# Softmax tiles of a two-block attention kernel stored as two halves, and a later place for some loads

## The chip, the cores and the metric

One NeuronCore of one Trainium2 chip runs the whole kernel. The metric is device time in microseconds (us) for one execution. The kernel before was run three times: 259.44, 259.83 and 260.8 us, median 259.83 us. Its engines are named as the profile names them: PE (TensorE matmul), PEld (its weight load), DVE (VectorE), ACT (ScalarE), POOL (GpSimd) and SP (SyncE, which here issues every DMA of the kernel).

## What is computed

Two attention blocks over 2048 tokens of width 640, with 32 heads of 20 elements, side by side in the output. All inputs are bfloat16.

```python
def _A_ref(x, wqkv, wo):          # block A: sliding window of 256 keys
    q, k, v = ...                 # x @ wqkv, cut in three, 32 heads of 20
    scores = jnp.einsum("bhqd,bhkd->bhqk", q, k) * (Dh ** -0.5)
    mask = (idx[:, None] - idx[None, :] >= 0) & (idx[:, None] - idx[None, :] < W)   # W = 256
    p = _softmax(jnp.where(mask[None, None], scores, -1e9), axis=-1)
    return einsum("bhqk,bhkd->bhqd", p, v) (heads joined) @ wo

def _B_ref(x, wqkv, wo):          # block B: linear attention
    pq, pk = phi(q), phi(k)       # phi(t) = where(t > 0, t + 1, exp(t)) + 1e-6
    kv = jnp.einsum("bhsd,bhse->bhde", pk, v)
    z = jnp.einsum("bhsd->bhd", pk)
    o = einsum(pq, kv) / (einsum(pq, z) + 1e-6)
    return (heads joined) @ wo
```

## The kernel before, in words

**Superblocks and tiles.** The 2048 tokens are cut into 4 superblocks s of 512 queries. Block A works on groups of 4 heads (8 groups g). The function `tiles_of` (L39) packs the needed parts of the banded score matrix of one superblock into score tiles of 128 keys by 4 heads by 512 columns: 16 tiles for superblock 0, 20 for each of the others, 76 in all, numbered 0 to 75. From superblock 1 on, five tiles serve two groups g and h = g+1, in this order: `first(g)`; `before(g)` with `middle(g)`; `last(g)` with `middle(h)`; `first(h)`; `before(h)` with `last(h)`. In a tile with two pieces, the first piece fills columns 0 to 255 of every head and the second columns 256 to 511. So the third tile of five holds, in one buffer, a half that group g needs (`last`) and a half that only group h needs later (`middle`, called "M").

**One tile** is made by `scores` (L753). PE multiplies keys and queries into a PSUM tile `S_ps` (L763; one buffer, half of PSUM). ACT takes the exponential of all 4 x 512 columns into the SBUF tile `p` (L781; five buffers). POOL then sets to zero what lies outside the window, with affine selects (L795): one of 128 columns a head for each "D" or "E" edge, and two of 256 columns a head for "M", the first of which writes another tile, `plow`, and the second `p` itself.

**values** (L806) multiplies a group's tiles with the values of block A: for every piece four matmuls (L822), one for each head j = 0 to 3, which run side by side in four column strips of the array and read `columns(p, j, ...)`. It is issued two tiles (LAG) after the group's last tile. Pieces of `first` are read as four runs of 64 columns with a step of 128 (`step=P`); all others as one run.

**Filling PE.** Between tiles, PE gets the dense matmuls of both blocks (projections, key sums, output products) from a plan written out by hand. Each entry has a due time t in tiles: `at(t0, t1, ...)` spreads the banks of a product over t0 to t1, `do(t, t, ...)` places a call. `fill_of` (L1058) sorts all entries by t, and the main loop (L1084) takes columns from that list as each tile gives it credit. In the profile tile i starts about 18 + 3 i us after the span's start (tile 27 at 97.1 us, tile 34 at 118.0 us). A load takes no PE columns, so moving one changes SP's order and nothing in the order of the other engines.

**SP's order** is the program's order, and SP stands still at an entry whose operand isn't ready. These calls matter below: `load_part` (L934, a DMA transpose of 128 tokens of x into `xA` or `xB`, 4 for a superblock, 160 KB each), `load_tok` (L535, 640 KB of block B's tokens), `keep_x` (L927, writes the transposed `xB`, 640 KB, to DRAM scratch `x_scr`), `again_x` (L930, reads it back), `late_load` (L969; "B", 0 is 800 KB of query weights into `wB`), and `moves` (L369): the projected queries and keys of a superblock are partly written to scratch (L375) and read back in another place (L384), 4 writes and 4 reads of 60 KB for each.

Each p buffer, as `scores` makes it:

```python
p_all = pp.tile([P, 4 * SB + 2], BF16, name="p")
p = p_all[:, 0 : 4 * SB].rearrange("p (j q) -> p j q", j=4)
```

Of the kernel before, what the change touches and what calls it, by code (L numbers as in the profile page):

```python
# [11 lines left out]
ACT = mybir.ActivationFunctionType  # L12
# [8 lines left out]
SB = 512  # L21
# [13 lines left out]
HALF = P // 2  # L35
LOW = 2 * P
# [46 lines left out]
def columns(t, j, col, n, step):  # L83

    if step == HALF:
        return t[:, j, col : col + n]
    u = col % step
    v = t[:, j, col - u : col - u + n // HALF * step].rearrange("p (b q) -> p b q", q=step)
    return v[:, :, u : u + HALF]


@with_exitstack
def kernel(
# [10 lines left out]
    nc = tc.nc  # L104
# [4 lines left out]
    scale = float(DH) ** -0.5  # L109
# [127 lines left out]
    def soon(fn, banks):  # L237
        posts.append((begun[0] + banks, fn))
        posts.sort(key=lambda p: p[0])

    def settle(all=True):
        while posts and (all or posts[0][0] <= begun[0]):
            posts.pop(0)[1]()
# [4 lines left out]
    def add_load(a=0, d=0):  # L248
        load["A"] += a
        load["D"] += d  # L250
# [71 lines left out]
    for c in range(KT):  # L322
        m = EXTRA * c
        while m < EXTRA * (c + 1):
            n = min(EXTRA * (c + 1) - m, DH - m % DH)
# [424 lines left out]
    def key(s, rel):  # L750
        return 4 * s + rel

    def scores(s, parts, selects):  # L753
        S_ps = sps.tile([P, 4, SB], F32, name="S_ps")
        p_all = pp.tile([P, 4 * SB + 2], BF16, name="p")
        p = p_all[:, 0 : 4 * SB].rearrange("p (j q) -> p j q", j=4)
        nc.scalar.activation(out=p_all[0:1, 4 * SB : 4 * SB + 1], in_=ident[0:1, 0:1], func=ACT.Copy)

        def product(g, kb, k0, k1, q0, n, col, step):
            kt = k_pad[kb // TPS]  # L760
            ko = (kb % TPS) * P
            for j in range(4):
                nc.tensor.matmul(  # L763
                    columns(S_ps[k0:k1], j, col, n, step),
                    lhsT=kt[32 * j : 32 * j + DH, g, ko + k0 : ko + k1],
                    rhs=q_pad[s][32 * j : 32 * j + DH, g, q0 : q0 + n],
                    start=True,
                    stop=True,
                    tile_position=(32 * j, k0),
                )  # L770

        for g, rel, q0, n, col, step in parts:
            if rel == "M":
                own = key(s, q0 // P)
                product(g, own, 0, HALF, q0, n, col, step)

                far = own - 2 if own >= 2 else own
                product(g, far, HALF, P, q0 + (HALF if own >= 2 else 0), n, col, step)
            else:
                product(g, key(s, rel), 0, P, q0, n, col, step)  # L780
        nc.scalar.activation(out=p, in_=S_ps[:], func=ACT.Exp, scale=scale)  # L781
        add_load(a=2080)
        low = None
        if any(kind == "M" for kind, _, _ in selects):
            low = pl_.tile([P, 4, LOW], BF16, name="plow")
        for kind, c0, n in selects:

            v = p[:, :, c0 : c0 + n].rearrange("p j (b q) -> p j b q", q=HALF)
            if kind == "M":
                lv = low[:, :, c0 - LOW : c0 - LOW + n].rearrange("p j (b q) -> p j b q", q=HALF)  # L790
                jobs = [(lv, v, 1, 0), (v, v, -1, -HALF - 1)]
            else:
                jobs = [(v, v, 1, HALF) if kind == "D" else (v, v, -1, -1)]
            for dst, src, sgn, base in jobs:
                nc.gpsimd.affine_select(  # L795
                    out=dst,
                    in_=src,
                    pattern=[[0, 4], [0, n // HALF], [sgn, HALF]],
                    compare_op=ALU.is_ge,
                    fill=0.0,  # L800
                    base=base,
                    channel_multiplier=-sgn,
                )
        return p, low

    def values(s, g, held):  # L806


        O_ps = dps.tile([P, SB], F32, name="dense")
        todo = []  # L810
        for (_, rel, q0, n, col, step), (p, low) in held:
            if rel == "M":
                own = key(s, q0 // P)
                todo.append((own, low, q0, n, col - LOW, step))
                if own >= 2:
                    todo.append((own - 2, p, q0 + HALF, n, col, step))
            else:
                todo.append((key(s, rel), p, q0, n, col, step))
        for i, (kb, p, q0, n, col, step) in enumerate(todo):
            at = (kb % TPS * H + 4 * g) * HV  # L820
            for j in range(4):
                nc.tensor.matmul(  # L822
                    O_ps[32 * j : 32 * (j + 1), q0 : q0 + n],
                    lhsT=v_flat[kb // TPS % 3][:, at + j * HV : at + j * HV + 32],
                    rhs=columns(p, j, col, n, step),
                    start=(i == 0),
                    stop=(i == len(todo) - 1),
                    tile_position=(0, 32 * j),
                    skip_group_check=True,
                )  # L830
        if turns[0] and g == 0:
            settle()

        T = tp.tile([P, SB // 32, 32], F32, name="T")
        nc.vector.transpose(out=T.rearrange("p b e -> p (b e)"), in_=O_ps[:])  # L835
        add_load(d=1500)
        if s not in norm_A:
            norm_A[s] = (
                np_.tile([P, SB // 32, P], BF16, name="N"),
                np_.tile([P, SB // 32, 32], BF16, name="Nr"),  # L840
            )
        N, Nr = norm_A[s]

        def rest():
            r = sp.tile([P, SB // 32, 1], F32, name="recA")
            nc.vector.reciprocal(out=r[:], in_=T[:, :, DH:HV])
            lo = g * DH
            for dst, a, b in ((N, lo, min(lo + DH, P)), (Nr, max(lo, P), lo + DH)):
                if a >= b:
                    continue  # L850
                at = a - P if dst is Nr else a
                nc.vector.tensor_tensor(  # L852
                    out=dst[:, :, at : at + b - a],
                    in0=T[:, :, a - lo : b - lo],
                    in1=r[:].to_broadcast([P, SB // 32, b - a]),
                    op=ALU.mult,
                )
            if lo < P <= lo + DH:
                oT_A[s] = op1.tile([P, KT, SB], BF16, name="oT")

                def turn(j):
                    quadrant = slice(32 * j, 32 * (j + 1))
                    nc.sync.dma_start_transpose(
                        out=oT_A[s][:, j, :].rearrange("p (b e) -> p b e", e=32),
                        in_=N[quadrant].rearrange("p b x -> p (b x)"),
                    )
                    turns[0] -= 1

                if s < NS - 1:
                    turns[0] = 4  # L870
                    for j in range(4):
                        soon(lambda j=j: turn(j), 2 + 2 * j)
            if g == NG - 1:
                nc.vector.transpose(
                    out=oT_A[s][:, KT - 1, :], in_=Nr.rearrange("p b e -> p (b e)")
                )

        later.append((begun[0], rest))
# [48 lines left out]
    def keep_x(s):  # L927
        nc.sync.dma_start(out=x_scr[s], in_=xB[s].rearrange("p k n -> p (k n)"))
# [73 lines left out]
    def at(t0, t1, gen, n):  # L1002
        for i in range(n):
            plan.append((t0 + (i + 0.5) / n * (t1 - t0), gen, i == n - 1))

    def do(t0, t1, fns):
        fns = list(fns)
        for i, fn in enumerate(fns):
            plan.append((t0 + (i + 0.5) / len(fns) * (t1 - t0), None, fn))
# [22 lines left out]
        at(t0, t1, b_keys(s), KT)  # L1032
    for half, t0, t1 in ((0, 16.4, 21.5), (1, 33.6, 39.2)):
        at(t0, t1, b_sums(half), KT + 2)
    for s, t in ((0, 6), (1, 11), (2, 23), (3, 24)):
        do(t, t, [lambda s=s: load_tok(s)])
    at(40.4, 42, b_kv(), 2)
    do(42.8, 44.8, [lambda c=c: kv_ready(c) for c in range(3)])
# [6 lines left out]
    for n, s, t0, t1 in (("A", 0, 44.5, 48.5), ("A", 1, 49.2, 54.2), ("B", 0, 55.2, 59.4),  # L1045
                         ("B", 1, 60.2, 64), ("A", 2, 64.4, 68.2), ("B", 2, 69, 73),
                         ("B", 3, 73, 76)):
        at(t0, t1, (a_out if n == "A" else b_out)(s), KT)
    for n, s, t0, t1 in (("B", 1, 5, 9), ("A", 2, 6, 12), ("B", 2, 14, 18), ("A", 3, 16, 24),
                         ("B", 3, 17, 22)):  # L1050
        parts(t0, t1, n, s)
    for s, t0, t1 in ((0, 2, 33.5), (1, 12, 38.5), (2, 20, 45.5), (3, 26, 51.2)):
        do(t0, t0, [lambda s=s: keep_x(s)])
        do(t1, t1, [lambda s=s: again_x(s)])
    for t, n, w in ((13, "B", 2), (20, "B", 0), (40.6, "A", A_wo), (42, "B", B_wo)):
        do(t, t, [lambda n=n, w=w: late_load(n, w)])

    def fill_of(events):  # L1058
# [25 lines left out]
    for i, (s, parts, selects, done) in enumerate(units):  # L1084
        p = scores(s, parts, selects)
# [60 lines left out]
```

## Time and profile before

| what | before |
| --- | --- |
| runs, median (range) | 259.83 us (259.44 to 260.8) |
| the profiled execution's own time | 260.06 us |
| its span, first to last instruction | 258.3 us |
| PE busy | 248.4 us, 96% of the span |
| ACT, DVE, POOL busy | 200.2, 176.9, 171.6 us |
| granted TensorE clock | 1.0 |
| bytes moved by DMA | 36.35 MB, mean 141 GB/s |

The profiled execution spends 1.8 us outside its span. Busy shares are of the span. A line number such as L822 is one of the kernel before. "Idle before" an instruction is the time in which its engine did nothing just ahead of it, and "<-" names what ended that time. The chain is the sequence of work that ended last, followed back from the end.

### The profile page before, as it was taken

The page shows a single profiled execution, that of the slowest core. Times are in us where ns is not written, and L with a number is a line of the kernel's source. Part 1 is how long each engine was busy: PE and PEld are TensorE (multiplying, and loading weights), DVE is VectorE, ACT ScalarE, POOL GpSimd, SP SyncE. Part 2 cuts the span into 40 slices and gives each one's busy share as a digit, 9 for nine tenths or more (in the row PEclk, how much of TensorE's full clock was granted, in tenths as well). Part 3 has the DMA queues.
Part 4 walks back from the last instruction along what each step waited for, and adds up shares of the span by engine and source line. Part 5 has one row for each costly group of instructions (what it writes and reads, how often), then busy time and mean ns, then how long its engine had stood idle before and what let it go on. Part 6 is the DMA issues. An engine that isn't in the chain of part 4 may idle for free.

```text
span 258.3 us, 10761 instructions
## 1 busy us (share of the span) xinstructions
PE 248.4 (96%) x4722; PEld 143.0 (55%) x4769; DVE 176.9 (68%) x308; ACT 200.2 (77%) x260; POOL 171.6 (66%) x211
## 2 busy tenths in 40 slices
PE   8999999999999999999999999999999999999995
PEld 7644446556555745555457555555556454555573
DVE  0435787786735457866645677699999879978662
ACT  3466878899777788988667887788889998988742
POOL 7214777767794866758495787949667694976800
PEclk9999999999999999999999999999999999999999
DMA  6995588789869592403474591622957486985715
GB/s 204 323 240 157 94 207 125 153 217 213 114 93 265 113 289 38 147 3 60 95 110 124 69 179 43 171 44 58 181 91 167 66 174 171 103 141 122 232 48 184
DMA packets 65012, 36.35 MB, mean 141 GB/s; under 512 B 48197, under 2 KB 63941, under 8 KB 64965
## 3 DMA queue, kind: packets, MB, share of 16 engines
q1 hardware_dynamic: 64965, 35.67, 65.2%
q8 instruction: 37, 0.61, 1.0%
q14 instruction: 10, 0.08, 0.1%
HBM read 14.42 MB, written 9.83 MB: 94 GB/s over the span
## 4 chain that ended last, share of the span: by engine, by line
PE 85%; POOL 6%; issue 4%; ACT 3%; DVE 1%; ACTq 0%; DVEq 0%
PE dense L277 44%; PE S_ps L763 11%; PE dense L546 9%; PE dense L822 8%; PE dense L412 8%; POOL p L795 4%; ACT p L781 2%; POOL plow L795 2%; PE dense L197 1%; PE dense L653 1%; PE dense L696 1%; PE dense L178 1%; PE dense L625 1%; ACT e L287 1%; DVE phi L294 1%
## 5 line engine op out<-in xcount | busy, mean ns | idle before, releaser
L781 ACT ACTIVATE p<-S_ps 128x2048 bf16<-128x2048 f32 x76 | 142.4, 1873 | 34.0 <-PE S_ps L763 33.2
L795 POOL TENSOR_SCALAR_AFFINE_SELECT p<-p 128x512 bf16<-128x512 bf16 (+1 forms) x152 | 123.2, 821 | 64.0 <-ACT p L781 58.7
L277 PE MATMUL dense<-xA,wqk 128*128 128x512 bf16 x183 | 47.2, 379 | 1.1 <-issue 0.6
L795 POOL TENSOR_SCALAR_AFFINE_SELECT plow<-p 128x1024 bf16<-128x1024 bf16 x32 | 38.7, 1210 | 2.2
L763 PE MATMUL S_ps<-qpad,kpad 20*64 20x64 bf16 (+3 forms) x1728 | 35.2, 213 | 0.4
L763 PEld LDWEIGHTS <-kpad 20*64 20x64 bf16 (+1 forms) x1728 | 17.4, 100 | 30.0 <-issue 25.5
L835 DVE STREAM_TRANSPOSE T<-dense 128x512 f32<-128x512 f32 x32 | 22.8, 712 | 12.5 <-PE dense L822 12.4
L277 PEld LDWEIGHTS <-wqk 128*128 128x128 bf16 x200 | 18.5, 98 | 20.6 <-issue 1.3
L291 DVE TENSOR_SCALAR e<-e 128x512 bf16<-128x512 bf16 x40 | 22.0, 550 | 10.7 <-ACT e L287 10.2
L294 DVE SCALAR_TENSOR_TENSOR phi<-dense,e 128x512 bf16<-128x512 f32 x40 | 27.7, 691 | 1.5
L412 PE MATMUL dense<-wA,xA 128*128 128x320 bf16 x160 | 28.4, 306 | 0.1
L822 PE MATMUL dense<-p,vA 128*32 128x64 bf16 (+2 forms) x1152 | 27.1, 223 | 0.5 <-POOL p L795 0.4
L277 PE MATMUL dense<-wB,xB 128*128 128x128 bf16 (+1 forms) x156 | 25.4, 297 | 0.8 <-issue 0.6
L287 ACT ACTIVATE e<-dense 128x512 bf16<-128x512 f32 x40 | 23.4, 594 | 2.5 <-PE dense L277 2.2
L277 PE MATMUL dense<-wo,oT 128*128 128x128 bf16 (+2 forms) x154 | 24.3, 296 | 1.0 <-issue 0.6
L546 PE MATMUL dense<-phi,tok 128*128 128x128 bf16 (+1 forms) x154 | 24.3, 296 | 0.7 <-issue 0.3
L277 PE MATMUL dense<-xB,wB 128*128 128x512 bf16 x90 | 24.2, 380 | 0.6 <-issue 0.3
L822 PEld LDWEIGHTS <-vA 128*32 128x32 bf16 x1664 | 22.2, 96 | 3.5 <-issue 1.3
L277 PE MATMUL dense<-wB,xA 128*128 128x512 bf16 (+1 forms) x156 | 23.4, 297 | 0.5 <-issue 0.3
L852 DVE TENSOR_TENSOR N<-T,recA 128x320 bf16<-128x320 f32 (+1 forms) x28 | 18.7, 668 | 3.3 <-DMA oT<-N 2.4
L732 DVE TENSOR_TENSOR tok<-tok,rden 128x640 bf16<-128x640 bf16 x16 | 19.8, 1236 | 0.0
L412 PEld LDWEIGHTS <-xA 128*128 128x128 bf16 x160 | 14.8, 100 | 9.0 <-issue 1.1
(68 smaller groups left out, 238.2 us busy)
## 6 DMA issues: line engine op xcount, KB each, us to landing
out_dram<-osb SPq DMA_DIRECT2D x7, 640.0 KB
x_scr<-xB SPq DMA_DIRECT2D x4, 640.0 KB
tok<-in_B_x_dram SPq DMA_DIRECT2D x4, 640.0 KB
xB<-x_scr SPq DMA_DIRECT2D x4, 640.0 KB
wB<-in_B_wqkv_dram SPq DMA_DIRECT2D x3, 800.0 KB
q_scr<-qpad SPq DMA_DIRECT2D x16, 60.0 KB
k_scr<-kpad SPq DMA_DIRECT2D x16, 60.0 KB
qpad<-q_scr SPq DMA_DIRECT2D x16, 60.0 KB
```

What stands on the lines that cost most here:

```text
L277: nc.tensor.matmul(dst, lhsT=lhs(kt), rhs=rhs(kt), start=(kt == 0), stop=(kt == KT - 1))
L287: nc.scalar.activation(out=view(e), in_=src, func=ACT.Exp)
L291: nc.vector.tensor_scalar(out=e[:], in0=e[:], scalar1=1e-6, scalar2=1.0 + 1e-6, op0=ALU.add, op1=ALU.min)
L294: nc.vector.scalar_tensor_tensor(out=dst, in0=src, scalar=0.0, in1=view(e), op0=ALU.max, op1=ALU.add)
L412: nc.tensor.matmul(ps[:, 0 : hh * DH], lhsT=xt[:, kt, tb * P : (tb + 1) * P], rhs=w_sb["A"][:, kt, i * hh * DH : (i + 1) * hh * DH], start ...
L546: nc.tensor.matmul(out, lhsT=lhs(x, pk)[:, tb, :], rhs=rhs(pk, tb), start=(i == 0), stop=(i == len(blocks) - 1),)
L732: nc.vector.tensor_tensor(out=vh, in0=vh, in1=rden_of[s][:, tb, :, :].to_broadcast([P, H, DH]), op=ALU.mult)
L763: nc.tensor.matmul(columns(S_ps[k0:k1], j, col, n, step), lhsT=kt[32 * j : 32 * j + DH, g, ko + k0 : ko + k1], rhs=q_pad[s][32 * j : 32 * ...
L781: nc.scalar.activation(out=p, in_=S_ps[:], func=ACT.Exp, scale=scale)
L795: nc.gpsimd.affine_select(out=dst, in_=src, pattern=[[0, 4], [0, n // HALF], [sgn, HALF]], compare_op=ALU.is_ge, fill=0.0, base=base, chan ...
L822: nc.tensor.matmul(O_ps[32 * j : 32 * (j + 1), q0 : q0 + n], lhsT=v_flat[kb // TPS % 3][:, at + j * HV : at + j * HV + 32], rhs=columns(p, ...
L835: nc.vector.transpose(out=T.rearrange("p b e -> p (b e)"), in_=O_ps[:])
```

## The change

The tile `p` keeps its size, but its columns are ordered differently. Before, head j had its 512 columns in one piece (head, column). After, columns 0 to 255 of all four heads come first, then columns 256 to 511 of all four heads (half, head, column). The exponential writes in the new order, the selects and the matmuls of `values` address it through the half; `plow` and `S_ps` are as before, so the list in `values` carries for each piece the function that addresses it. Besides, entries of the plan get other due times.

```diff
+def columns_p(t, j, col, n, step):
+    if step == HALF:
+        return t[:, col // LOW, j, col % LOW : col % LOW + n]
+    v = t[:, :, j, :].rearrange("p a (b q) -> p a b q", q=step)
+    return v[:, :, :, col : col + HALF]
...
-        p = p_all[:, 0 : 4 * SB].rearrange("p (j q) -> p j q", j=4)
+        p = p_all[:, 0 : 4 * SB].rearrange("p (a j q) -> p a j q", a=2, j=4)
...
-        nc.scalar.activation(out=p, in_=S_ps[:], func=ACT.Exp, scale=scale)
+        nc.scalar.activation(
+            out=p.rearrange("p a j q -> p j a q"),
+            in_=S_ps.rearrange("p j (a q) -> p j a q", a=2),
+            func=ACT.Exp,
+            scale=scale,
+        )
...
-            v = p[:, :, c0 : c0 + n].rearrange("p j (b q) -> p j b q", q=HALF)
+            v = p[:, c0 // LOW, :, c0 % LOW : c0 % LOW + n].rearrange(
+                "p j (b q) -> p j b q", q=HALF
+            )
...
-                todo.append((own, low, q0, n, col - LOW, step))
+                todo.append((own, low, q0, n, col - LOW, step, columns))
                 if own >= 2:
-                    todo.append((own - 2, p, q0 + HALF, n, col, step))
+                    todo.append((own - 2, p, q0 + HALF, n, col, step, columns_p))
             else:
-                todo.append((key(s, rel), p, q0, n, col, step))
-        for i, (kb, p, q0, n, col, step) in enumerate(todo):
+                todo.append((key(s, rel), p, q0, n, col, step, columns_p))
+        for i, (kb, p, q0, n, col, step, of) in enumerate(todo):
...
-                    rhs=columns(p, j, col, n, step),
+                    rhs=of(p, j, col, n, step),
...
-    for s, t in ((0, 6), (1, 11), (2, 23), (3, 24)):
+    for s, t in ((0, 6), (1, 11), (2, 24.2), (3, 28.2)):
         do(t, t, [lambda s=s: load_tok(s)])
...
-    for n, s, t0, t1 in (("B", 1, 5, 9), ("A", 2, 6, 12), ("B", 2, 14, 18), ("A", 3, 16, 24),
-                         ("B", 3, 17, 22)):
+    for n, s, t0, t1 in (("B", 1, 5, 9), ("A", 2, 6, 12), ("B", 2, 14, 18), ("B", 3, 19, 25),
+                         ("A", 3, 25.5, 33.5)):
         parts(t0, t1, n, s)
-    for s, t0, t1 in ((0, 2, 33.5), (1, 12, 38.5), (2, 20, 45.5), (3, 26, 51.2)):
+    for s, t0, t1 in ((0, 2, 33.5), (1, 12, 38.5), (2, 26.2, 45.5), (3, 30.2, 51.2)):
         do(t0, t0, [lambda s=s: keep_x(s)])
         do(t1, t1, [lambda s=s: again_x(s)])
-    for t, n, w in ((13, "B", 2), (20, "B", 0), (40.6, "A", A_wo), (42, "B", B_wo)):
+    for t, n, w in ((13, "B", 2), (32.2, "B", 0), (40.6, "A", A_wo), (42, "B", B_wo)):
         do(t, t, [lambda n=n, w=w: late_load(n, w)])
```

## Prediction, made before the changed kernel was run

> **What bounds the kernel now.** I read the page's busy row first, then the chain, the waits of PE, PE's timeline around the longest ones, POOL's part of the chain there, and last the stretches that tell what the DMA engines did.
>
> ```profile
> span 258.3 us, 10761 instructions
> PE 248.4 (96%) x4722; PEld 143.0 (55%) x4769; DVE 176.9 (68%) x308; ACT 200.2 (77%) x260; POOL 171.6 (66%) x211
> PE 85%; POOL 6%; issue 4%; ACT 3%; DVE 1%; ACTq 0%; DVEq 0%
> ```
>
> PE is busy nearly throughout, at the full granted clock, and 85% of the chain is PE. So only two things can move the end: PE's own work, or the few places where PE stands. All of PE's waits:
>
> ```profile
> PE dense L277 <- issue: 2.5, 16, 0.2
> PE dense L197 <- DVE osb L193: 1.1, 1, 1.1
> PE dense L822 <- POOL p L795: 0.4, 2, 0.3
> PE dense L546 <- issue: 0.3, 2, 0.2
> PE dense L277 <- DVE wB L264: 0.3, 1, 0.3
> ```
>
> Columns: who waited for whom, us in all, times, longest. No row names a DMA. The 1.1 us is the start. What remains with a releaser that the change touches is POOL's, 0.4 us in two waits; the wait is longer than that row says, because a matmul counts as busy till its modelled end. PE's timeline at one of the two places, and the chain there (start us, us, what):
>
> ```profile
> 211.13 0.22 PE L822 MATMUL dense<-p,vA 128*32 128x64 bf16 x5
> 211.62 0.29 PE L822 MATMUL dense<-p,vA 128*32 128x64 bf16 x7 [0.26 <-POOL p L795]
> ```
>
> ```profile
> 208.74 1.16 POOL plow L795
> 209.90 0.06 issue
> 209.96 1.62 POOL p L795
> 211.58 0.04 issue
> 211.62 0.29 PE dense L822 x7
> ...
> 225.29 1.62 POOL p L795
> 226.91 0.04 issue
> 226.96 0.29 PE dense L822 x7
> ```
>
> The reader is to see that the stop falls inside a set of four. `values` of an even group issues 48 matmuls for `first`, `before` and `middle`, and then the 64-column piece of `last`, heads 0 to 3. Four of the row x5 are the end of `middle`, the fifth is head 0 of `last`; head 1 starts only when a select of 1.62 us ends. That length is the form of 1024 elements (0.67 us is the 512 form's median), so PE waits for the second select of "M", which writes columns 256 to 511 of the same tile. These matmuls read columns 0 to 63. Head 0 needn't wait for it (its columns lie ahead of all that "M" writes), but heads 1 to 3 lie between the "M" columns of head 0 and those of head 3: the wait is taken for the whole stretch of memory from the select's first to its last element. In every `values` of an even group from superblock 1 on, the 49th and the 50th matmul each carry a wait on POOL's semaphore, which agrees.
>
> **The change, part one: the halves.** In the new order "M" writes elements 1024 to 2047 of a buffer and `last` reads from 0 to 1023: the stretches no longer overlap, and heads 1 to 3 wait for the "D" select alone, which at this place ended at 208.66 us, 2.5 us before they are issued.
>
> *What goes.* By the starts of single matmuls, the 50th follows the 49th by 6 to 8 ns in nine of the twelve `values` concerned, and by 458 ns (at 211.62 us), 377 ns (226.96) and 163 ns (166.35) in the other three. Less 7 ns each: 0.45 + 0.37 + 0.155 = 0.975 us. What is late next: after 226.96 and after 211.62 the chain goes on through PE, ACT's e and p, all started by PE itself (at 211.62 DVE had been idle for 1.40 us, waiting for these matmuls), so these two gains should be kept. After 166.35 PE waits for DVE at 180.67 (0.11 us over the usual spacing) and at 185.92 (the row of 0.3); DVE is busy 92% of 170 to 180 us, so I count half of 0.155 as lost. Sum: 0.45 + 0.37 + 0.08 = 0.90 us.
>
> *What is added.* (a) The exponential writes in 8 runs of 256 instead of one of 2048. No row shows that; the nearest are ACT's copies of 320 columns: 437 ns into `vA` (16 runs of 20), 426 ns into `wB` (one run). So at most 11 ns an exponential; from the other side, the 76 exponentials themselves vary from 1850 to 1879 ns, so a gain of up to 29 ns isn't excluded. I take nothing: the next tile's score matmuls start 0.3 to 0.7 us after the exponential's end in most tiles and within 0.13 us only in six early ones; 6 x 0.011 = 0.07 us at worst. If the cover went in all tiles, 76 x 0.011 = 0.8 us. (b) POOL's selects: the 1024 form takes 1152 ns at its shortest both on `p` (4 runs) and on `plow` (one run), so the new runs cost nothing; and POOL has no PE wait left to lengthen. (c) `values` reads `first` as 2 x 2 runs of 64 with two steps instead of 4 with one. Not in the trace; the sets of four now start about 107 ns apart for 256 columns, as do the score matmuls of 256 columns that read one run, so breaks cost nothing in these rows, and single sets lie between 93 and 111 ns. 64 sets: between -0.9 and +0.26 us; I take nothing, as both nearest rows say. (d) A head's step of 256 elements is that of `plow` now: 195 ns a matmul against 194 from `p`. Nothing. (e) Waits: pieces of `first` span both halves and so wait for both their edge selects, as now; their tile is at least three tiles old. No wait is added.
>
> **Part two: the moved entries.** Moved: B's parts of superblock 3 (4 transposes of 160 KB, t 17-22 to 19-25), `load_tok` 2 and 3 (640 KB each, 23 and 24 to 24.2 and 28.2), A's parts of superblock 3 (4, 16-24 to 25.5-33.5), `keep_x` 2 and 3 (640 KB, 20 and 26 to 26.2 and 30.2), and B's query weights (800 KB, 20 to 32.2). They pass one thing on SP: the scratch write of superblock 2's queries, due near t 26.5, at which SP now stands from 90.63 to 100.32 us. A's four parts, `load_tok` 3, `keep_x` 3 and the weights then stand behind it. POOL and ACT issue no DMA and have no order to change.
>
> SP's time behind the wait: 1.6 us of writes, 4 transposes of 1.25, 4 reads of 0.35 with 1.8 us of waits for the writes, 4 others of 0.5: 11.8 us, from 100.3 to 112.1, ahead of the key write for which it waits until 118.06 anyway. Bytes: 640 + 640 + 640 + 800, with the unmoved 480 of query scratch and 640 of `again_x`, 3.84 MB.
>
> ```profile
> 64.00:76.00 12.00, 11.42 (x182) 5.81 (x184) 7.55 (x15) 9.05 (x12) 9.82 (x11) 1.00 0.78 103
> 76.00:100.00 24.00, 23.63 (x546) 14.26 (x549) 13.75 (x28) 18.82 (x22) 14.91 (x20) 1.00 0.72 189
> 100.00:118.00 18.00, 17.68 (x354) 9.74 (x358) 13.30 (x23) 16.10 (x22) 13.38 (x16) 1.00 0.24 66
> ```
>
> The last two columns are the DMA engines' busy share and GB/s. From 76 to 100 us the same kinds of transfer took 0.72 x 24 = 17.3 us of DMA time for 0.189 x 24 = 4.5 MB, so 3.84 MB take 14.8 us and are down at 115.1 us, in a stretch that is 76% free now. First uses, by PE's timeline: `tok` 3 just after 117.25 us (with some 1.1 MB up to and with it, down at 108), `xA` of superblock 3 at 126.28, the weights at 139.70. B's parts end before 90 us and are used from 99 on, the last near 108. So nothing is late; and as PE waits for no DMA now, nothing is gained either: 0 us. The cover is 9 to 11 us; gone, each us of it is a us on the path.
>
> A row and a rule: SP's next transfers are issued here while earlier ones are under way (`tok` is issued 0.5 us after a transpose). The Trainium skill, in "DMA: Bandwidth & Descriptors" under "Two DMAs through the same engine are not ordered", has it that descriptors of one queue of a DMA engine start in order. By it the query reads of 60 KB, which come between the large loads, start behind these and could land up to 14.8 us later, near 120 us; their first use is in tile 49 at 162.4 us, so the sum is the same, and if they overtook, the same too. No row of this case shows the order of starts.
>
> **Sum.** 260.06 - 0.90 = 259.16 us for the profiled execution. That stands 0.23 us over the median of the runs, so against the median 259.83 - 0.90 = **258.9 us**, 0.35% less. About 0.5% (1.3 us, so 258.5 and 261.1) is what a measurement of this kernel can tell from no change.
>
> **Rivals.** *It doesn't do what it says.* The wait of heads 1 to 3 stays, because it hangs on POOL's count and not on the stretch: 259.8 us. Against: head 0 in the same buffer goes on before the "M" select ends.
>
> *More than I count.* In other executions the "M" select (1152 to 1612 ns in this one) ends later in some of the nine `values` that now just pass; three more stops of 0.37 us would make 257.8 us. Against: the runs' median is below the profiled execution.
>
> *Slower: the bunch comes late.* Behind the query write 3.2 MB go ahead of and with the last part of `xA`. At the 103 GB/s of 64 to 76 us, where most transfers were such transposes, this takes 31.1 us, to 131.4 us; PE reaches the query projection of superblock 3 at 126.28 and stands 5.1 us: 264.0 us. It decides below 3.2 MB / 26 us = 123 GB/s. For: four transposes are among them. Against: 189 GB/s right after, with the same kinds.
>
> *Slower: the new read of `first`.* Should the two-step read halve PE's pace, 64 x 0.107 = 6.8 us come on the path: 265.7 us. Against: (c).
>
> **Chances.** The forecast 0.60 (own range 258.3 to 259.5), no effect 0.13, more 0.11, bunch late 0.09, slow read 0.07. Of the forecast's 0.60 some 0.13 lies below 258.5. So faster by over 0.5%: 0.11 + 0.13 = 0.24; within: 0.47 + 0.13 = 0.60; slower: 0.09 + 0.07 = 0.16. The range leaves out the two slow cases and takes in the bounds of (a) and (c): 257.8 to 260.9 us.
>
> **What would show it.** Right: no stop at the 50th matmul of `values` and no PE wait on POOL; exponentials still near 1877 ns; sets of `first` still 107 ns apart; SP issues A's parts after 100 us, and no DMA among PE's waits. Wrong: the stop is still there (first rival); `dense<-xA,wqk` near 126 us or `dense<-phi,tok` near 117 us idle for a DMA (bunch); wider sets (slow read); or PE's waits for DVE grow by what POOL's lose, so that the time stays.

## The result and the profile after

The changed kernel takes 258.13 us (median of 14 runs, 257.97 to 259.13), the kernel before 259.83 us in the same comparison: a ratio of 0.993, 95% interval 0.9907 to 0.9952. That is 1.70 us less (1.2 to 2.4 by the interval), where 0.90 was forecast. 258.13 lies in the whole range given, 257.8 to 260.9, but 0.17 us below the forecast's own range, 258.3 to 259.5. Beside other kernels on one chip it came to 258.57 against 259.94 us (0.9954, 0.9933 to 0.9975; run e8 below), 1.37 us less (0.6 to 1.7). So the gain is about 1.4 to 1.7 us; the 0.90 lies below the first interval and inside the second. Lines move by 10 to 17: L277 becomes L287, L291 L301, L795 L812, L822 L839.

The page after: span, busy row of the engines, and the chain by engine.

```profile
span 256.9 us, 10798 instructions
PE 252.3 (98%) x4769; PEld 142.7 (56%) x4769; DVE 177.7 (69%) x308; ACT 199.8 (78%) x260; POOL 170.4 (66%) x211
PE 96%; DMA 2%; ACT 0%; DVE 0%; SPq 0%; issue 0%; ACTq 0%
```

POOL is gone from the chain. PE's busy time seems to have grown by 3.9 us, but read the counts: 4769 matmuls here, 4722 before, while the weight loads were 4769 both times. The page before lacked 47 matmul records, and the row "issue: 2.5, 16" of its waits was mostly their holes (a hole is exactly one matmul, 0.216 us, wide). So busy times of PE can't be compared here, but the weight loads can, one for one.

All waits of PE after:

```profile
PE dense L207 <- DVE osb L203: 1.1, 1, 1.1
PE dense L287 <- DVE wB L274: 0.3, 1, 0.3
```

The wait on POOL is gone, and so is a wait on DVE of 0.2 us at 64.31 us. The profile before has a row for it, which the prediction's list of all waits left out:

```profile
PE dense L546 <- DVE phi L294: 0.2, 1, 0.2
```

PE's timeline at the place where it had stood at 211.62 us:

```profile
210.40 0.21 PE L839 MATMUL dense<-plow,vA 128*32 128x64 bf16 x4
210.43 0.34 PE L839 MATMUL dense<-p,vA 128*32 128x64 bf16 x12
```

The end of `middle` and all of `last` are now one row of 12, with no stop behind the fifth. SP's timeline (start, us, issue):

```profile
102.40 1.20 SPq L956 DMA_TRANSPOSE xA<-in_A_x_dram  x1
...
110.52 2.17 SPq L956 DMA_TRANSPOSE xA<-in_A_x_dram  x1
```

A's parts go out from 102.4 to 112.7 us, behind the query write (99.80), as forecast, and PE waits for none of them.

**Where the time came from.** PE's weight loads stand in the same order in both kernels, so the start of the nth in one less its start in the other shows where the two draw apart. The table gives that difference to the kernel before, in us (negative: earlier), at thirteen places named by the time before. A step between two columns is a gain or a loss made there.

| kernel | 10 | 50 | 70 | 160 | 170 | 179 | 183 | 209 | 213 | 218 | 225 | 229 | 250 |
| --- | --- | --- | --- | --- | --- | --- | --- | --- | --- | --- | --- | --- | --- |
| after | -0.19 | -0.19 | -0.49 | -0.52 | -0.67 | -0.67 | -0.78 | -0.70 | -1.14 | -1.27 | -1.27 | -1.63 | -1.47 |
| e1, halves only | -0.86 | -0.86 | -1.15 | -1.21 | -1.37 | -1.36 | -1.47 | -1.38 | -1.83 | -1.60 | -1.60 | -1.96 | -1.96 |
| e2, loads only | -0.59 | -0.59 | -0.59 | -0.62 | -0.62 | -0.62 | -0.62 | -0.61 | -0.61 | -0.61 | -0.61 | -0.61 | -0.61 |
| e3, wait back | -0.37 | -0.37 | -0.02 | -0.01 | -0.15 | -0.15 | -0.25 | -0.24 | -0.35 | -0.46 | -0.46 | -0.42 | -0.41 |
| e4, memset | -0.63 | -0.58 | -0.77 | -0.80 | -0.95 | -0.95 | -1.02 | -1.02 | -1.47 | -1.62 | -1.62 | -1.98 | -1.98 |
| e5, POOL waits | -0.60 | -0.60 | -0.59 | -0.63 | -0.77 | -0.77 | -0.77 | -0.77 | -1.21 | -1.34 | -1.34 | -1.71 | -1.65 |
| e6, other order | -0.04 | -0.04 | -0.59 | -0.59 | -0.73 | -0.73 | -0.84 | 0.04 | -0.40 | -0.54 | -0.54 | -0.77 | -0.77 |
| e7, parts latest | -0.61 | -0.61 | -0.91 | 5.44 | 5.30 | 5.30 | 5.19 | 5.22 | 4.78 | 4.63 | 4.63 | 4.27 | 4.27 |
| e8, after again | -0.36 | -0.36 | -0.66 | -0.69 | -0.83 | -0.83 | -0.94 | -0.92 | -1.36 | -1.13 | -1.13 | -1.50 | -0.85 |

The first column is an execution's own: the first 10 us differ by up to 0.9 us whatever the kernel. They hold the first loads, and the time up to which a matmul of 128x128 takes 314 ns instead of 219 (it is over by 4.1 us in e1 and lasts past 5.3 us in the kernel before). No such difference stays in the medians (e2 is the clearest case). From 10 us on, most steps repeat to some hundredths of a us. In "after" they are: at 166, 211.6 and 227 us -0.15, -0.44 and -0.36, together 0.95 us, the three stops of the prediction; from 50 to 70 us -0.30 and at 180 us -0.11, together 0.41 us, which no step of the prediction had; at 215 us -0.13; at 202 us +0.08; between 229 and 250 us +0.16; and some hundredths. The sum from 10 us on is 1.28 us. What the medians have beyond it, 0.1 to 0.4 us, no trace assigns.

### The profile page after: what moved, and what is told of

It reads as the page before. It is cut to its first block, busy times and chain, and to the rows that moved or that the text cites. A ratio compares the mean times of both kernels' runs of the same rounds, so it can differ in the third digit from the quotient of the medians.

```text
span 256.9 us, 10798 instructions
## 1 busy us (share of the span) xinstructions
PE 252.3 (98%) x4769; PEld 142.7 (56%) x4769; DVE 177.7 (69%) x308; ACT 199.8 (78%) x260; POOL 170.4 (66%) x211
## 4 chain that ended last, share of the span: by engine, by line
PE 96%; DMA 2%; ACT 0%; DVE 0%; SPq 0%; issue 0%; ACTq 0%
PE dense L287 53%; PE S_ps L773 12%; PE dense L556 10%; PE dense L839 10%; PE dense L422 9%; DMA wA<-in_A_wqkv_dram 2%; PE dense L663 1%; PE dense L706 1%; PE dense L635 1%; PE dense L906 0%; PE dense L188 0%; DVE wB L274 0%; ACT vA L272 0%; SPq L182 0%; ACT osb L272 0%
## 5 line engine op out<-in xcount | busy, mean ns | idle before, releaser
L791 ACT ACTIVATE p<-S_ps 128x2048 bf16<-128x2048 f32 x76 | 142.4, 1873 | 32.4 <-PE S_ps L773 31.7
L812 POOL TENSOR_SCALAR_AFFINE_SELECT p<-p 128x512 bf16<-128x512 bf16 (+1 forms) x152 | 122.5, 829 | 65.9 <-ACT p L791 63.7
L287 PE MATMUL dense<-xA,wqk 128*128 128x512 bf16 x200 | 50.0, 380 | 0.0
L812 POOL TENSOR_SCALAR_AFFINE_SELECT plow<-p 128x1024 bf16<-128x1024 bf16 x32 | 39.6, 1237 | 0.0
L301 DVE TENSOR_SCALAR e<-e 128x512 bf16<-128x512 bf16 x40 | 22.1, 554 | 11.5 <-ACT e L297 10.9
L287 PEld LDWEIGHTS <-wqk 128*128 128x128 bf16 x200 | 18.5, 98 | 20.6 <-issue 1.3
L839 PE MATMUL dense<-p,vA 128*32 128x64 bf16 (+2 forms) x1152 | 26.7, 223 | 0.0
L287 PE MATMUL dense<-wB,xB 128*128 128x512 bf16 (+1 forms) x160 | 25.9, 300 | 0.0
L287 PE MATMUL dense<-xB,wB 128*128 128x512 bf16 x100 | 25.8, 380 | 0.0
L287 PE MATMUL dense<-wo,oT 128*128 128x512 bf16 (+2 forms) x160 | 25.3, 300 | 0.3 <-DVE wB L274 0.3
L556 PE MATMUL dense<-phi,tok 128*128 128x512 bf16 (+1 forms) x160 | 25.1, 300 | 0.0
L287 PE MATMUL dense<-wB,xA 128*128 128x512 bf16 (+1 forms) x160 | 24.2, 300 | 0.0
L839 PEld LDWEIGHTS <-vA 128*32 128x32 bf16 x1664 | 22.1, 96 | 2.7 <-issue 0.7
L272 ACT ACTIVATE osb<-dense 128x512 bf16<-128x512 f32 (+1 forms) x25 | 13.9, 568 | 6.9 <-PE dense L287 4.6
```

Source lines behind the costliest of these rows:

```text
L287: nc.tensor.matmul(dst, lhsT=lhs(kt), rhs=rhs(kt), start=(kt == 0), stop=(kt == KT - 1))
L301: nc.vector.tensor_scalar(out=e[:], in0=e[:], scalar1=1e-6, scalar2=1.0 + 1e-6, op0=ALU.add, op1=ALU.min)
L556: nc.tensor.matmul(out, lhsT=lhs(x, pk)[:, tb, :], rhs=rhs(pk, tb), start=(i == 0), stop=(i == len(blocks) - 1),)
L791: nc.scalar.activation(out=p.rearrange("p a j q -> p j a q"), in_=S_ps.rearrange("p j (a q) -> p j a q", a=2), func=ACT.Exp, scale=scale,)
L812: nc.gpsimd.affine_select(out=dst, in_=src, pattern=[[0, 4], [0, n // HALF], [sgn, HALF]], compare_op=ALU.is_ge, fill=0.0, base=base, chan ...
L839: nc.tensor.matmul(O_ps[32 * j : 32 * (j + 1), q0 : q0 + n], lhsT=v_flat[kb // TPS % 3][:, at + j * HV : at + j * HV + 32], rhs=of(p, j, c ...
```

## Experiments

After the result my theory was: the 0.41 us, and the 0.13 at 215 us, came from POOL. Its second select of a tile no longer waits for the first one's end, starts earlier, and lets DVE instructions that collide with it end earlier, for which PE had waited. The rival: the moved loads did it.

**e1_halves_only**: the changed kernel with the due times of before.

```diff
-    for s, t in ((0, 6), (1, 11), (2, 24.2), (3, 28.2)):
+    for s, t in ((0, 6), (1, 11), (2, 23), (3, 24)):
...
-    for s, t0, t1 in ((0, 2, 33.5), (1, 12, 38.5), (2, 26.2, 45.5), (3, 30.2, 51.2)):
+    for s, t0, t1 in ((0, 2, 33.5), (1, 12, 38.5), (2, 20, 45.5), (3, 26, 51.2)):
```

> The halves alone, with the due times of before. My theory after the result: all of the gain comes from the halves, 0.96 us from the three stops of the 50th matmul of values and 0.58 us from four waits of PE for DVE (0.15 at 55.5, 0.19 at 64.3, 0.10 at 180.7, 0.14 at 215.3 us of before), which went because POOL's second select of a tile starts about 0.115 us earlier (it no longer waits for the first one's end). So the time is that of the changed kernel, 258.1 us, no PE wait on POOL, and the gap ahead of a tile's second select is 0 ns instead of 68. Rival, the moved loads took away the waits for DVE: 258.9 us, the four waits for DVE are there as before.

Measured 258.4 us, 0.9948 (0.9926 to 0.997). Its steps up to 213 us are those of "after"; at 215 us it loses 0.23 instead of gaining 0.13 (why is read under e5).

**e2_loads_only**: the kernel before with the due times of after.

```diff
-    for n, s, t0, t1 in (..., ("A", 3, 16, 24), ("B", 3, 17, 22)):
+    for n, s, t0, t1 in (..., ("B", 3, 19, 25), ("A", 3, 25.5, 33.5)):
...
-    for t, n, w in ((13, "B", 2), (20, "B", 0), ...):
+    for t, n, w in ((13, "B", 2), (32.2, "B", 0), ...):
```

> The due times of after alone, with p as before. My theory: 259.8 us as before, the three stops of 0.16 to 0.46 us on POOL and the four waits for DVE as before; A's parts are issued after 100 us and nothing is late. Rival, the loads bring 0.6 us: 259.2 us, stops on POOL there, waits for DVE gone.

Measured 260.04 us, 1.0009 (0.9991 to 1.0026), and a flat line in the table: at its thirteen places PE keeps its distance within 0.03 us. The three stops at the 50th matmul are there (159, 459 and 377 ns). The rival falls: moving the loads does nothing in this kernel, neither good nor bad.

**e3_wait_given_back**: one matmul more, which takes up the old wait.

```diff
+                if j == 0 and s > 0 and g % 2 == 0 and i == len(todo) - 2:
+                    nc.tensor.matmul(O_ps[0:32, q0 : q0 + 1], lhsT=none[:],
+                                     rhs=p[:, 1, 0, 0:1], start=False, stop=False, ...)
```

> The changed kernel with one more matmul in each of the twelve values of an even group from superblock 1 on: behind head 0 of the first piece of last, a matmul of a weight tile of zeros with one column of the M half, which adds 0 and waits for the second M select as heads 1 to 3 did before. My theory: the stops of before come back where the select ends late, near 166, 211 and 227 us, together about 0.9 us, so 259.0 us; POOL's gaps of 0 ns and the absence of the waits for DVE stay. Rival, the stop was not what cost the time (its gain is lost or won elsewhere): 258.2 us.

Measured 259.33 us, 0.9986 (0.9963 to 1.001). PE's timeline in it:

```profile
210.89 0.23 PE L841 MATMUL dense<-p,vA 128*32 128x64 bf16 x5
211.26 0.16 PE L851 MATMUL dense<-p,none 128*32 128x1 bf16 x1
211.27 0.29 PE L841 MATMUL dense<-p,vA 128*32 128x64 bf16 x7
```

The stop is back in the old place, in front of the matmul that reads the "M" half: 0.34 us here and 0.41 us at 226.5. The third, at 166, isn't (3 ns): POOL is ahead of its old time. So 0.75 of the 0.9 us expected came back by this way. The rest of its loss is a hole of 0.59 us in PE's work at 62.8 us for which the profile shows no releaser ("issue"); in e1 a smaller loss (0.16 us) stands at another matmul of the same `values`. What they are wasn't tried and stays open.

**e4_pool_memset**: something for POOL to do between the selects.

```diff
+        for at, (kind, c0, n) in enumerate(selects):
+            if at == 1:
+                nc.gpsimd.memset(idle[:], 0.0)
```

> The changed kernel with a memset of one column (about 0.10 us by the 128x1 memsets at the start) on POOL between a tile's first and second select, 76 in all, which gives POOL back about the 0.115 us that its second select lost. My theory: PE's waits for DVE come back, up to 0.58 us, so about 258.6 us, and DVE's e<-e that end with a select are longer again by about 0.1 us; no stop of PE on POOL. Rival, POOL's earlier second select does nothing for PE: 258.1 us.

Measured 258.53 us, 0.9965 (0.9948 to 0.9982). POOL's timeline at 52 us:

```profile
52.10 0.67 POOL L814 TENSOR_SCALAR_AFFINE_SELECT p<-p 128x512 bf16<-128x512 bf16 x1 [1.17 <-ACT p L792]
52.71 0.10 POOL L804 MEMSET idle<- 128x1 bf16 x1
52.76 1.15 POOL L814 TENSOR_SCALAR_AFFINE_SELECT plow<-p 128x1024 bf16<-128x1024 bf16 x1
```

The memset of 0.10 us costs only 0.04 us, since neighbours without a dependency overlap: the second select starts 0.66 us behind the first, against 0.62 in "after" and 0.73 before. With a third of the delay given back, a third of the gain went: the steps are -0.19 and -0.07 instead of -0.30 and -0.11. The full price forecast for it was wrong, because I had put the memset in at its own duration; the step at 215 us stayed.

**e5_pool_waits_again**: the delay in full, by the dependency itself.

```diff
+                if len(made) == 2:
+                    tc.add_manual_dep(made[1].ins, made[0].ins.name,
+                        mybir.DependencyInfo(mybir.DependencyClass.Sync, mybir.DependencyReason.DATA), ...)
```

> The changed kernel with one dependency more: a tile's second select waits for its first, as it did before the change; PE's matmuls keep what the halves gave them. My theory: the second select starts 0.115 us later again (0.73 us behind the first instead of 0.62), PE's four waits for DVE come back in full (0.58 us; the memset of e4, which cost 0.05 of the 0.115 us, gave back 0.17 us of them), no stop on POOL: 258.7 us, 0.9955 of before. Rival, the four waits went for another reason: 258.1 us, 0.993.

Measured 258.68 us, 0.995 (0.9931 to 0.9969). In the table the steps from 50 to 70 us and at 180 us are gone to the last hundredth, the three of POOL's stops are whole. So 0.41 us belong to POOL's own wait. "After", e1, e7 and e8 all show these two steps (about -0.30 and -0.11), e2 and e5 neither. The fourth, at 215 us, does not come back (-0.13), while e1 and e8 lose 0.23 there: my theory was wrong for it. The times can't tell 0.41 us apart (0.2% against intervals of 0.4%); the verdict is the profiles', of one execution for each kernel.

The wait that went is in the rows of the second select where it writes `plow`. The last number is POOL's idle time ahead of all 32, before and after:

```profile
L795 POOL TENSOR_SCALAR_AFFINE_SELECT plow<-p 128x1024 bf16<-128x1024 bf16 x32 | 38.7, 1210 | 2.2
L812 POOL TENSOR_SCALAR_AFFINE_SELECT plow<-p 128x1024 bf16<-128x1024 bf16 x32 | 39.6, 1237 | 0.0
```

How POOL's wait reaches PE can be read at 53 us. POOL's and DVE's timelines, before:

```profile
52.68 0.67 POOL L795 TENSOR_SCALAR_AFFINE_SELECT p<-p 128x512 bf16<-128x512 bf16 x1 [1.10 <-ACT p L781]
53.41 1.15 POOL L795 TENSOR_SCALAR_AFFINE_SELECT plow<-p 128x1024 bf16<-128x1024 bf16 x1
```

```profile
53.62 1.09 DVE L291 TENSOR_SCALAR e<-e 128x512 bf16<-128x512 bf16 x1 [0.81 <-ACT e L287]
```

After:

```profile
52.48 0.67 POOL L812 TENSOR_SCALAR_AFFINE_SELECT p<-p 128x512 bf16<-128x512 bf16 x1 [1.24 <-ACT p L791]
53.10 1.15 POOL L812 TENSOR_SCALAR_AFFINE_SELECT plow<-p 128x1024 bf16<-128x1024 bf16 x1
```

```profile
53.43 0.97 DVE L301 TENSOR_SCALAR e<-e 128x512 bf16<-128x512 bf16 x1 [0.81 <-ACT e L297]
```

And in e5:

```profile
52.08 0.67 POOL L812 TENSOR_SCALAR_AFFINE_SELECT p<-p 128x512 bf16<-128x512 bf16 x1 [1.12 <-ACT p L791]
52.81 1.15 POOL L812 TENSOR_SCALAR_AFFINE_SELECT plow<-p 128x1024 bf16<-128x1024 bf16 x1
```

```profile
53.02 1.09 DVE L301 TENSOR_SCALAR e<-e 128x512 bf16<-128x512 bf16 x1 [0.81 <-ACT e L297]
```

The same DVE instruction takes 0.28 us at its shortest. Here it begins inside POOL's select into `plow` and ends 0.15 us after that select's end in all three: 54.71 after 54.56, 54.40 after 54.25, 54.11 after 53.96. It waits for POOL while it counts as busy. The Trainium skill, in "SBUF — State Buffer" under "Who interferes with whom", says that VectorE and GpSimd share one pair of ports, that a `tensor_scalar` in a two-port mode takes it, and that whoever issues first has it for the whole instruction while the other is blocked. The trace agrees, with 0.97 to 1.09 us instead of 0.28; that it ends 0.15 us behind the select and not a whole 0.28 is not explained by any run. So a select that starts 0.115 us sooner lets DVE go 0.115 us sooner, and PE, which at 55.5, 64.3 and 180.7 us waited for DVE, gains it up to what it had waited. At 64.3 the step is 0.19 us, because two more `e<-e` ahead of it are shorter, by 0.07 and 0.12 us. At 180.7 the instruction that got shorter is DVE's product `tok<-tok,rden`: 1.76 us before, 1.65 in "after", 1.77 in e5. The select starts sooner because its stretch of the buffer no longer touches that of the one ahead: the gap between the two was 0.07 us of idle time and is 0 now, and the rest is the overlap of neighbours.

The step at 215 us is another meeting of DVE and POOL. PE waits there for a `phi` of DVE. Two instructions ahead of that `phi`, DVE makes the product `N<-T,recA`. POOL's select and that product, in "after" and in e1:

```profile
211.25 0.66 POOL L812 TENSOR_SCALAR_AFFINE_SELECT p<-p 128x512 bf16<-128x512 bf16 x1
211.85 0.49 DVE L869 TENSOR_TENSOR N<-T,recA 128x320 bf16<-128x320 f32 x1
```

```profile
211.27 0.67 POOL L812 TENSOR_SCALAR_AFFINE_SELECT p<-p 128x512 bf16<-128x512 bf16 x1
211.28 0.99 DVE L869 TENSOR_TENSOR N<-T,recA 128x320 bf16<-128x320 f32 x1
```

In "after", e6 and e7 the product begins in the last 0.14 us of a select or less, and takes 0.49 us, its shortest. In the other seven executions it begins with 0.26 to 0.66 us of a select left and ends 0.33 us behind that select's end: it takes 0.88 us in the kernel before and in e2, 0.59 to 0.77 in e3, e4 and e5, and in e1 and e8, where it begins just behind a select's start, 0.99 and 0.97. Those two are the ones that lose. Counted from the start of the "M" select ahead, the product comes only about 0.1 us later in them than in "after", so which way it goes hangs on a tenth of a us; no run moved that on purpose.

**e6_selects_without_gap**: in tiles with an "M" piece, `plow` first, then the edge, then "M" in place.

```diff
+        if low is not None:
+            todo = [todo[-2], *todo[:-2], todo[-1]] if selects[-1][0] == "M" else [
+                todo[0], *todo[2:], todo[1]
+            ]
+        for dst, src, sgn, base, n in todo:
+            nc.gpsimd.affine_select(...)
```

> The changed kernel with the selects of a tile with an M piece in another order: M's select into plow first, then the edge, then M's select in place, so that the last one doesn't wait for the end of the one just ahead of it. POOL should lose the 68 ns gap of these 32 tiles. My theory: PE has hardly a wait left that POOL could take away (0.06 us at 63.8, the 0.3 for wB), so 258.1 us; and the edge ends some 1.2 us later, still ahead of the 49th matmul. Rival, POOL's ends set more than the trace shows: 257.8 us or less.

Measured 259.0 us, 0.9967 (0.9953 to 0.998): neither. It keeps all the steps, some of them larger or smaller, but between 192 and 194 us PE loses 0.9 us (it stands at -0.84 us at 183 and +0.04 at 209). DVE's timeline there, after and in e6:

```profile
190.01 1.01 DVE L742 TENSOR_TENSOR tok<-tok,rden 128x640 bf16<-128x640 bf16 x1
```

```profile
190.46 1.63 DVE L742 TENSOR_TENSOR tok<-tok,rden 128x640 bf16<-128x640 bf16 x1
```

The gaps did go, but the selects now fall elsewhere under DVE's work: the same product takes 0.62 us longer, another one two instructions ahead 0.48, and DVE empties PE's banks so much later. In this execution, which DVE instruction meets which select matters more than 2 us of POOL's gaps. By the medians e6 is 0.4 us slower than the changed kernel on the same chip (e8), which the intervals don't tell apart.

**e7_parts_latest**: A's parts due at t 34 to 36.4.

```diff
-                         ("A", 3, 25.5, 33.5)):
+                         ("A", 3, 34, 36.4)):
```

> The changed kernel with A's four parts of superblock 3 due at t 34 to 36.4 instead of 25.5 to 33.5, behind the key scratch write for which SP waits until about 117.6 us. By my sum SP issues the last part near 126 us and it lands near 128, while PE wants all four near 125.7: PE stands some 2 us at the first query bank of superblock 3, so about 260 us. Rival, the cover is larger than I think (or PE finds other work): 258.1 us.

Measured 264.15 us, 1.0159 (1.0128 to 1.019). PE's waits, and the stretches around it (busy of PE, PEld, DVE, ACT, POOL, then PE's granted clock, DMA share, GB/s):

```profile
PE dense L287 <- DMA xA<-in_A_x_dram: 3.7, 1, 3.7
```

```profile
120.00:125.00 5.00, 5.00 (x97) 2.50 (x90) 3.33 (x6) 3.88 (x4) 2.39 (x4) 1.00 0.69 107
125.00:129.10 4.10, 0.51 (x3) 0.02 (x1) 0.69 (x1) 0.04 (x1) 1.28 (x2) 0.90 0.59 119
129.10:135.00 5.90, 5.82 (x112) 2.64 (x112) 2.25 (x4) 2.56 (x3) 2.40 (x3) 0.50 1.05 169
```

SP issues the last part at 126.06 us, as worked out; by the chain it lands 2.88 us later, at 128.94, instead of 128, and PE stands 3.7 us, till 129.18. Then its clock is granted at half for 5.9 us, and it falls back by another 2.3 us. So the slower rival of the prediction is a real mechanism with the place named, and it is dearer than a us for each us late.

**e8_changed_again**: the changed kernel unaltered.

> The changed kernel itself, beside the three others on one chip: 258.1 us, 0.993 of before. It shows how far a second profile of the same program differs at the places that the others are judged by: no stop on POOL, no wait of PE for DVE over 0.1 us but that for wB.

Measured 258.57 us, 0.9954 (0.9933 to 0.9975). Its steps are those of "after", but for 215 us, and for the end, where it loses 0.65 us from 229 to 250 us:

```profile
PE dense L287 <- DMA xA<-tok: 0.5, 1, 0.5
```

These are among the last transposes of block B's quotients (L746 on SP), wanted at 238 us by a PE that arrives some 1.1 us earlier than before. The 0.16 us of "after" have the same cause at a later one of them: a weight load waits for `xA<-tok` at 243 us. None of the others loses more than 0.06 us there. A part of the gain can be given back there; how often, these executions don't say.

## Why the prediction came out as it did

- **What bounds the kernel**: right. PE's work is the same; only its waits changed. But "All of PE's waits" was not all: the row of 0.2 us on DVE's `phi` was left out, and it is one of the three waits that made the 0.41 us.
- **The wait for the whole stretch of memory**: right, at all three places, 0.95 us by the table against 0.975 read from the trace before. e3 shows it by putting the wait back alone, at two of the three places (0.75 us).
- **"After 166.35 PE waits for DVE at 180.67 ... so I count half of 0.155 as lost"**: wrong. It was kept in full, because the wait for DVE at 180.67 went as well.
- **(b), "the new runs cost nothing; and POOL has no PE wait left to lengthen"**: this is the step that failed. The runs do cost nothing (at its shortest the 1024 form takes 1153 ns on `p` and 1148 on `plow`), but I looked at a select's duration alone. The chain that I showed has "issue" pieces of 0.06 us between selects of one tile: POOL waited there for itself, on the same overlapping stretches as PE, and the halves took that wait away too. Through DVE it reached PE and made 0.41 us, a term that the sum hadn't; e5 gives it back. The last sign of being wrong, that PE's waits for DVE grow, had the right engine and the wrong direction.
- **(a), (c), (d), (e)**: right. The exponential takes 1873 ns on average, as before; the 256-column matmuls of `values` 278 ns, as before, and by the starts of single matmuls their sets of four lie 110 ns apart in the median in both kernels (109 to 121, so the 107 of the prediction was a little low); matmuls from `p` 194 ns and from `plow` 195.
- **Part two, 0 us**: right, by e2. The cover of 9 to 11 us was real: by the trace of "after" A's last part landed at 116.7 us, 9 us ahead of its use at 125.76, and e7 used the cover up and PE stood. That a us late is a us on the path was wrong: 3.7 us of standing came to 5.6 us of time (264.15 against 258.57; 6.4 us by e7's row in the table), for the clock's sake.
- **The rivals**: the wait did go; the loads weren't late; the new read isn't slow. "More than I count" (257.8 us) lies nearer to the 258.13 us than the forecast does, while the 1.37 us of the second comparison lie between the two; but it was not its mechanism (more stops at the 50th matmul): it was another wait of another engine.
- **The number**: that 258.13 us lies in the range is in part luck. The 0.95 and the 0.41 us that the traces show would make 258.5 us, still inside the forecast's own range. 258.13 lies below it by what no trace assigns, and inside the whole range because its lower end, 257.8, was there for more stops, which didn't come.

## What to carry to other kernels

When a layout makes two accesses stop overlapping, look for every instruction that touches the buffer and not only at the one whose stop is in the chain: here POOL's waits for itself, 0.07 us each and of no account by themselves, held up DVE and through it PE. On an engine that shares its ports, a busy time is no duration: compare an instruction with its own shortest, and see which neighbour's end it shares. And judge changes of half a us by aligning the two traces instruction by instruction from behind the start, since the first 10 us alone move a span by up to 0.9 us.

## What the hardware did that I had not expected

- DVE's `e<-e` of 512 columns, 0.28 us at its shortest, ended 0.15 us after POOL's select at 54 us in three kernels. DVE's `N<-T,recA`, 0.49 us at its shortest, ended 0.33 us after a select in seven executions.
- Two POOL instructions with no dependency overlap by about 0.05 us, so that a memset of 0.10 us between them cost 0.04 us.
- A stop of PE of 3.7 us was followed by 5.9 us at half the granted clock and cost another 2.3 us.
- A transpose of 160 KB landed 2.9 us after SP began to issue it in e7 (126.06 to 128.94 us), with DMA engines 59% busy, and the last of the same four 6.2 us after it in "after" (110.52 to 116.7 us).
